# Transposes of two chunks moved from TensorE to VectorE and DRAM, in a rewritten instruction order

## The chip, the cores and the metric

The kernel runs on one core of a Trainium2 chip. The metric is the device time of one execution in microseconds (us). Three runs of the kernel before took 554.64, 554.66 and 555.55 us; their median is 554.66 us.

## The reference

Sequence length 2048, width 512, 32 heads of 16, hidden width 1376, everything in fp32. The block is an attention part followed by a mixing part:

```python
mod = silu(c) @ w_mod                      # six rows: sa, ca, ga, sb, cb, gb
h  = layernorm(x) * (1 + ca) + sa
q, k, v = split_heads(h @ wqkv)
phi(t) = [softmax(t @ w_phi), softmax(-t @ w_phi)]
o  = phi(q) (phi(k)^T v) / (phi(q) . sum(phi(k)))
x  = x + ga * (o @ wo)                     # called x2 below
h  = layernorm(x) * (1 + cb) + sb
g  = gelu(layernorm(h) @ w1)
x1 = h + shift(g) @ w2                     # quarters of g moved by +1, -1, +2, -2 rows
y  = x1 + gelu(layernorm(x1) @ w3) @ w4
out = x + gb * y
```

## The kernel before, in words

The 2048 rows are 16 tiles of 128 rows, and eight chunks (0 to 7) of two tiles each. A product of fp32 accuracy is made of three fp32r matmuls: every operand is split into a rounded part `hi` and a remainder `lo` (`hi_lo`, L483: one instruction makes `hi`, one subtraction makes `lo`), and `three` (L474) emits hi·hi, hi·lo and lo·hi.

There are three stages. First come the q, k and v projections of all rows, with the sums over k and v. Then `phase_a(c)` (L909) runs for each chunk: it finishes the attention, multiplies by `wo` (the pieces called o below: 6 matmuls of 128x512 for half of a tile), adds x, forms two layer norms with ScalarE (`moments`, `shift_of`), writes the normalized rows to the tile `n`, turns them with TensorE into the tile `nT` (`to_T`, L861), and multiplies `nT` by w1 (the pieces g: 24 matmuls of 128x256, two for each chunk). Its gelu goes to the tile `sh`, and `mix(c)` (L1009) multiplies shifted columns of `sh` by w2 (the pieces x: 3 matmuls of 128x512, four for each tile) and stores x1. Last come w3 and w4 in blocks of 512 rows (`block(s)`, L1208): the pieces u (6 or 12 matmuls) and v, and then the pieces b of `down_steps`.

`to_T` is where the change sits. For one tile of 128 rows it lets TensorE transpose four squares of 128x128 into one PSUM tile `pt` (`transp`, L477; matmuls of line L480) and makes `nT` from `pt` with `hi_lo`. The pieces n below are such sets of four transposes.

The stage of w3 already turns rows without TensorE: `normed(c)` (L1118) has ScalarE write the normalized rows with their columns permuted, VectorE transposes every 32x32 block of a tile (`turn`, L760), `store_rows` (L1103) puts the tile into a DRAM buffer, and `load_turned` (L1107) reads that buffer back with four DMAs, one for each group of 32 partitions, into the tile `bL`. Its line in the profile is L1111, that of the stores L1104.

Nothing schedules at run time. Each engine works off its instructions in order. The order comes from a list written out by hand into the file, `ORDER` (L40): it names 2801 planned operations by number, with a letter where an operation goes to another engine than its first (A ScalarE, V VectorE, G GpSimd). A second table, `SLOT` (L166), gives each tile its buffer. All DMAs quoted here are issued from one queue, SP, in the list's order; an issue that waits holds back all that stand behind it.

Read back into names, TensorE's part of the list around the change is this (chunk 5's pieces are g5, and the tiles 10 and 11 are its rows; chunk 6 has the tiles 12 and 13, chunk 7 the tiles 14 and 15; n12 and n14 name the transposes of chunks 6 and 7; x3 means three pieces in a row):

```
... x8 o14 u01 n10 x8 o14 o14 o14 | g5 n12 n12 g5 g6 g6 | x9 x10*3 x9*3 u00*2 x10 u00
    x11*4 u01 n14 n14 u01 v00 x12*2 g7 u02 g7 ...
```

Of the kernel before, what the change touches and what calls it, by code (L numbers as in the profile page):

```python
# [29 lines left out]
SHIFT = (1, -1, 2, -2)  # L30

# [9 lines left out]
    "0 3 35 6 52 2 42 50 5 54 56 36 237 23 7 37 11 1 12 13 14 17G 31 10 38 86G 19 39 43 88 8 44 18 9 49V 84 27 40 "  # L41
    "45 16 4 46 41V 51 47 87 53 48G 100 55 85G 92 15G 57 62 58 236 59 67 60 96 61 24 63V 68 81 64V 69 32 65V 70 "
    "151 20 239 33V 214 66 89 150 21V 28 90 34 332 22 101 230 29 25 30 93 227 238 26 216 97 240 71 241 225 102V "
    "82G 104 242 94V 243 153 95 83G 91 244 152 78 72 75 103 215G 113 246 233 106 154 98 248G 105 333 156 99 155 "
    "231V 107 157 334 311 219 140 158 245 316 217G 160 115 159 161 247V 79 162V 313 226G 114 228 412 168 142 163 "
    "169 218G 305 132 116 164 222 170 413 229G 165V 171 477 166 172 232G 117 167 254 73 249 141 335 80G 133V 300 "
    "255 769 195 135 109 76G 108 256V 143 220 312G 542 257 74G 478 134 144 110 182 145 136G 302 336 337 146 250V "
    "314 251V 173 184 338 221G 183 223 415 315 319 339 224G 185 301 203 252 174 77G 196 111 306 253 340 480 197 "
    "234 191 112G 198 303 204 118 258 342 317G 344 205 119 199G 341 268 138 343 120 479 308 206 318G 137 414 139 "
    "345 270 304G 350 416 259 346V 417 269 121G 201 175 320 347V 418 271 235G 208 127 200 351V 128 207 352V 321G "  # L50
    "202 193 786 261 353 176 419 787G 309 307G 788 354 177 543 260 178 209 420 186 348V 608 279 310G 481 679 179 "
    "422 421 482 424G 349 483 262 322 149G 423 187 122 323V 264 484 355 324 263 485 188 192 325 770G 487 486 545 "
    "180 773G 189 273 181G 326 265 123 396 544 489 430 357 124 194 356 190G 125 327 488 266 400 425 358 281 426 "
    "126 328 211 546 547 431 771 607 213G 777 129 610 282V 404 329 130 359 284 360 495 131V 490 272 267G 147 432V "
    "667 427V 148 408 210 283 428 212 361 491 285G 364 548 433 362 496 429 397G 774 434 792 789 286 435 405 287 "
    "775 549 492 288 274 550 609 776 409G 932 493 497V 552 275 373 554 790 276G 437 498 791 436 877 410 673 611 "
    "499 612 331 494 363G 444 551 398 365 553 366 367 399G 509 368 793 772 369 794 401 894 780 778 406 781G 438 "
    "613 881G 555 782 500 446 556 895G 445 557 878G 896 440 447 558 280 297 439 560 277 449 407 614 882 615 510 "
    "448 402 299 617 619 879 520 278 393 891 616 668 892G 370 618 411G 893 455 374 371 670 783 511 658 372G 824 "
    "897 521 441 561 562 512 883G 375 563 880G 1480 779 450 395G 502 442 625 564 620 626 296 559 403G 627 298 501 "  # L60
    "704 514 392 451 565 376 443G 621V 888 503 628 818 885 655 513 629 452G 674 504 394 567 622 505 474G 566 623 "
    "515 574 456 568 898G 624 569 886 900 1146 453 1247 576 671 887 901G 570 575 661 476G 330 516 506 630 571 "
    "889G 577 517G 639 507 578 454 508 579 539 518 572 541G 631 640 580 473 519 475 573G 702 705 538 540 385 641 "
    "675G 926 632 890 581 1140 633 604G 902 289 634 387 635 899 386 659 725 582G 642 884 662 731 388 644 377 660G "
    "643 636 390 606G 389 645 391 648 378 291 637 784 638G 379 785 290 585 380 649 795 703 653G 646 292 583 664 "
    "586 663 293 656 647 294 657 295 683 584 1481 381 684 797 603 685 605 672 383 652 457 708 1033 706 799G 458 "
    "650 709 707 665 382 460 669G 384 459 903 710 465 862 711 461G 651 712 713 714 796 717G 462 798 654 466 587 "
    "680 800 463 715G 464 467 718 801G 681 468 588 522 590 682 469G 716 802 905 719 523 720 907G 524 530 721 803 "
    "589 984 471 525 723 722 470 526G 804 472 908 732 531 805 533 591G 527 686 806 528 532 529 807 724 808G 592 "
    "906 593 594 733 904 687 810G 1001 1482 809 726 1004 1010 534G 734 727 689 735 688 736 812 728 536 694 909G "  # L70
    "811 737 738 739 729V 1005G 740 742 730 1007 535 741 744 813 690G 743 595 1012 816 814 695 745 910 666G 746 "
    "747 537 815 748 985G 676 817 819 749 1008G 911 691 1011 692 750 820 912 693 1014G 751 697 753 1039 913 696 "
    "825 752 914 757 821 1119 1002G 754 915 822 1015 758 916G 755 826 759 1003 756 1009 760 1006 918G 827 765 917 "
    "828 830 831 698G 919 832 920 833 835 1117 921 834 837 761 922 1016G 836 924 838 823 677 829 923 839 840 1013 "
    "1123G 699 927 841 1017 700 933 925 842 701 843 1018 1124 1226 986G 845 928 844 850 1019 988G 1020 1118 846 "
    "987G 851 1121G 852 847 1021 934 1224 848 853 849 1022 854 935 766 1023G 1122 762 763 929 936 1025G 1024 938 "
    "937 939 858 930 1120 767 931 764G 940 1026 998 768G 941 855 1027 943 1305 992 1028 942 945 865 1029 1228G "
    "1125 944 1031 866 596 1030 1386 867 856 1126 946 859 1034 857G 995 1032 860 1127 947 1128 861G 1040 949 1129 "
    "1091 1227 948 678G 1198 1041 1484 950 597 951 598 1035 1130G 1042 952 954 1229 953 868 958 1036 864 955 863 "
    "1132G 1043 871 869 956 959 1131 870 1045 972 1037 1047 1038 872 996G 957 1044 960 873 1133 599G 1486 1046 "  # L80
    "973 1048 1050 989 1388 974 1221 961 1049 1134 1052 993G 1135 975 1051 1230G 600 1053 601 874 1225 602 1054 "
    "966 1055 997 1108 1222G 1231 1136 1109G 1056 1223 1232 994 1483G 1138 1233 1234 962 1057 1235 999G 976 1307 "
    "1058 1236 1137 967 1239G 1387 968 1110 1060 1141 1059 1000 1114 1139 1061 977 1237G 875 1065 1147 1240 963 "
    "1111 1306 990G 1062 964 1066 1063 1487G 1148 991 1238 1215 876 1067 1092G 1142 1064 1112G 1068 1309G 1149 "
    "1113 1241 1253 1143 1242 1073 1308 1243 1245 1150 1216G 1244 1152 1151 1246 1093G 1566 1311 1217 978 1074 "
    "1069 1115 1094 1153 1154 1565 1116 965 1159 1155 1102 1156 1144 969G 1096 1160 1145 1248 1070 1583 1157 "
    "1097G 1075 1158 1071 1103G 1254 1098 1312 1161 1078 1162 1104 970 971 1622 979 1163 1072 980 1392 1567 1249 "
    "1164 1494 1165 1393 1218 1495G 1167 1255 1166 1568 1531 1310 1168 1219G 981 1250 1569 1076G 1099 1220 1169 "
    "1172 982 1079 1100G 1251 1170V 983 1080 1570 1313 1390G 1561 1314 1173 1171 1252 1081 1174 1101 1256 1571 "
    "1082 1315 1175 1186 1572 1584 1257 1316 1573 1623 1391 1180 1259 1077 1574 1485G 1576 1389 1261 1488G 1317 "  # L90
    "1575 1578 1318G 1577 1176 1083 1579 1586 1181 1260 1580 1266 1581 1258 1489 1585 1320 1514 1085 1084 1587 "
    "1588 1334 1086 1562 1262 1182 1187 1319 1263 1177 1192 1183G 1178 1321 1582 1087 1589 1179G 1188 1394 1563 "
    "1395 1264 1322 1492 1564G 1498 1323 1396 1397 1328 1088 1324 1516 1184 1326 1491G 1325 1189 1590 1398 1591 "
    "1089 1329 1490G 1593 1267 1090 1595 1399G 1327 1335 1592 1265 1500 1415 1594 1190 1268 1330 1270 1401G 1400 "
    "1191 1269 1193 1598 1271 1336 1272 1402 1599 1782 1499G 1331 1403 1337 1404 1493G 1506 1194 1273 1596 1409 "
    "1338 1185 1501G 1274 1332V 1597 1195 1340 1275 1405V 1781 1293 1279G 1496 1196 1294 1515G 1406 1197 1603 "
    "1295 1407V 1333 1600 1601 1276 1604G 1342 1408 1416 1784 1602 1341 1636 1339 1532 1343 1621 1783 1344 1345 "
    "1800 1280 1785 1517G 1347 1508 1296 1786 1346 1417 1281 1497G 1348 1787 1282 1410 1788 1277V 1278 1789 1349 "
    "1351 1350 1411 1297 1504 1298 1418 1791 1352 1793 1353 1412 1355 1354 1360G 1419V 1356 1413V 1518G 1283 1420 "
    "1790 1792 1796 1202 1361 1284 1794 1095G 1547 1357 1799 1421 1287 1362 1212G 1795 1105 1363 1285G 1358 1509 "  # L100
    "1359 1802 1549 1213 1106 1214 1364 1548G 1288 1797 1801 1107 1414 1286G 1803 1627 1804 1507G 1289 1368 1805 "
# [1286 lines left out]
```

## Time and profile before

| | |
|---|---|
| median of three runs | 554.66 us |
| profiled execution, whole | 554.69 us |
| profiled execution, span from first to last instruction | 552.9 us |
| TensorE matmuls | 544.9 us busy, 4498 instructions |
| VectorE | 488.6 us busy |
| ScalarE | 351.7 us busy |
| GpSimd | 344.5 us busy |
| bytes moved by DMA | 124.90 MB |

A matmul's busy time includes its latency, and neighbours overlap. So a run of matmuls is read from the start of one piece to the start of the next. The chain of waits gives such pieces back to back: start, length, engine, output tile, line, and the number of instructions. In the view of one tile, an answer gives minimum, median and maximum of a duration in ns; the line on landing gives minimum, median and maximum of the time from a DMA's issue to its completion in us.

### The profile page before, as it was taken

Reading aid. Unit: us, or ns where it says so; the run is one execution under the profiler, and the core shown is the slowest. Engines: PE = TensorE matmul, PEld = TensorE weight load, DVE = VectorE, ACT = ScalarE, POOL = GpSimd, SP = SyncE. Lnnn points to the kernel's source line nnn. Section 1 sums busy time; section 2 is a strip of 40 time slices with the busy share of each in tenths; the row PEclk is TensorE's granted clock in tenths of the full one; section 3 lists DMA queues with packets and bytes.
Section 4 is the critical chain, followed back from the end, with each engine's and each line's share of the span. In section 5 each row is a group of like instructions: output and inputs, shape, how many; then the busy total and the mean of one; then the engine's idle time right before and its main releaser. Section 6 shows DMA issues by size and latency. Waiting matters only on the chain.

```text
span 552.9 us, 12370 instructions
## 1 busy us (share of the span) xinstructions
PE 544.9 (99%) x4498; PEld 488.1 (88%) x4498; DVE 488.6 (88%) x903; ACT 351.7 (64%) x828; POOL 344.5 (62%) x351
## 2 busy tenths in 40 slices
PE   8999999999989999999999999999999999999997
PEld 7888788878767788888889898999999999999996
DVE  3999999899999999999998878987888868896886
ACT  2899898834436788969888877866434543434540
POOL 2499985979599999978886545234150434254442
PEclk9999999999999999999999999999999999999999
DMA  8982544537736766869987878986689673872022
GB/s 323 392 277 89 175 170 137 176 112 248 205 118 226 249 195 206 275 235 319 292 275 270 242 257 301 339 356 231 284 248 347 245 284 97 264 286 80 25 92 95
DMA packets 63749, 124.90 MB, mean 226 GB/s; under 512 B 7140, under 2 KB 26852, under 8 KB 59592
## 3 DMA queue, kind: packets, MB, share of 16 engines
q1 hardware_dynamic: 63400, 124.04, 66.4%
q8 instruction: 35, 0.57, 0.4%
q14 instruction: 26, 0.21, 0.1%
q10 hardware_dynamic: 288, 0.07, 0.1%
HBM read 89.74 MB, written 34.35 MB: 224 GB/s over the span
## 4 chain that ended last, share of the span: by engine, by line
PE 86%; DVE 7%; POOL 3%; DMA 2%; issue 1%; ACT 0%; DVEq 0%; POOLq 0%
PE pp L471 36%; PE pa L471 27%; PE ac L471 20%; PE pt L480 2%; DVE pz L442 2%; DVE q L442 2%; DMA mod<-in_wmod 1%; PE kva L471 1%; POOL qe L420 1%; DVE pT L762 1%; POOL ez L420 1%; POOL e L420 1%; DVE ez L418 1%; DMA const<-in_c 1%; DVE pp L437 0%
## 5 line engine op out<-in xcount | busy, mean ns | idle before, releaser
L471 PE MATMUL pp<-w,hh 128*128 128x512 f32 x576 | 138.8, 397 | 0.0
L471 PEld LDWEIGHTS pp<-w,hh 128*128 128x128 f32 x576 | 106.7, 188 | 26.1 <-issue 1.6
L471 PE MATMUL pa<-bH,wq 128*128 128x256 f32 x840 | 106.7, 281 | 0.0
L471 PE MATMUL ac<-w,gg 128*128 128x256 f32 x840 | 106.6, 281 | 0.0
L471 PEld LDWEIGHTS ac<-w,gg 128*128 128x128 f32 x840 | 103.4, 189 | 1.1
L471 PEld LDWEIGHTS pa<-bH,wq 128*128 128x128 f32 x840 | 103.1, 189 | 0.9
L471 PE MATMUL pp<-w,sh 128*128 128x512 f32 x192 | 49.4, 399 | 0.0
L471 PE MATMUL pa<-nT,w 128*128 128x256 f32 x384 | 48.3, 282 | 0.8 <-DVE nT L418 0.7
L471 PEld LDWEIGHTS pa<-nT,w 128*128 128x128 f32 x384 | 46.8, 188 | 2.5 <-DVE nT L418 1.2
L471 PE MATMUL pp<-w,oT 128*128 128x512 f32 x192 | 47.4, 395 | 0.0
L471 PEld LDWEIGHTS pp<-w,oT 128*128 128x128 f32 x192 | 35.4, 188 | 8.1 <-DVE oT L418 0.7
L401 ACT ACTIVATE gg<-cu 128x256 fp32r<-128x256 f32 (+1 forms) x56 | 19.1, 359 | 35.1 <-PE ac L471 19.7
L471 PEld LDWEIGHTS pp<-w,sh 128*128 128x128 f32 x192 | 34.6, 188 | 7.5 <-issue 0.8
L588 POOL TENSOR_TENSOR rs<-mv,const 128x2 f32<-128x2 f32 x31 | 23.8, 769 | 25.3 <-ACT mv L595 23.7
L401 ACT ACTIVATE cu<-pa 128x512 f32<-128x512 f32 (+1 forms) x42 | 21.5, 519 | 27.6 <-PE pa L471 22.3
L420 POOL TENSOR_TENSOR gg<-cu,gg 128x128 fp32r<-128x128 f32 (+1 forms) x26 | 15.8, 615 | 33.2 <-ACT gg L401 13.9
L420 POOL TENSOR_TENSOR ez<-e,const 128x1024 f32<-128x1024 f32 x12 | 29.2, 2433 | 5.2 <-DMA dram<-qe 5.1
L401 ACT ACTIVATE gg<-sg 128x512 fp32r<-128x512 f32 x38 | 23.1, 624 | 14.0 <-POOL sg L420 6.0
L420 POOL TENSOR_TENSOR e<-e,q 128x1024 f32<-128x1024 f32 x15 | 28.8, 1938 | 0.4 <-DVE q L418 0.2
L418 DVE TENSOR_TENSOR gg<-cu,gg 128x256 fp32r<-128x256 f32 (+1 forms) x54 | 22.1, 416 | 7.6 <-PE ac L471 4.6
L418 DVE TENSOR_TENSOR gg<-sg,gg 128x512 fp32r<-128x512 f32 x36 | 26.0, 722 | 3.0 <-PE ac L471 1.5
L420 POOL TENSOR_TENSOR ke<-ke,k 128x1024 f32<-128x1024 f32 x14 | 27.2, 1952 | 1.2 <-DVE k L445 1.2
(214 smaller groups left out, 1211.5 us busy)
## 6 DMA issues: line engine op xcount, KB each, us to landing
wq<-dram SPq DMA_DIRECT2D x32, 1024.0 KB, 7.8
dram<-ws SPq DMA_DIRECT2D x35, 256.0 KB, 3.1
xl<-in_x SPq DMA_DIRECT2D x32, 256.0 KB, 4.1
dram<-qe SPq DMA_DIRECT2D x16, 512.0 KB, 3.7
e<-dram SPq DMA_DIRECT2D x64, 128.0 KB, 3.2
raw<-in_w SPq DMA_DIRECT2D x18, 256.0 KB, 3.7
mod<-in_wmod SPq DMA_DIRECT2D x16, 256.0 KB, 5.2
dram<-xl SPq DMA_DIRECT2D x16, 256.0 KB, 3.0
```

The costliest lines, as they stand in the source:

```text
L401: nc.scalar.activation(o(), i(), func, **kw)
L418: dve = ("DVE", 71 + 1.04 * o.n + 90 * (isps(a) and isps(b)), lambda: nc.vector.tensor_tensor(o(), a(), b(), op=op))
L420: pool = ("Pool", cost, lambda: nc.gpsimd.tensor_tensor(o(), a(), b(), op=op))
L442: plan.op("DVE", 65 + 1.04 * a.n + 110 * isps(o), lambda: nc.vector.tensor_reduce(o(), a(), axis=AX.X, op=op), [o], [a])
L471: nc.tensor.matmul(o(), a(), b(), start=s, stop=e, **kw)
L480: nc.tensor.transpose(o(), i(), ident())
L588: plan.op("Pool", 540 + 10 * m, lambda: nc.gpsimd.tensor_tensor(r(), v(), mhalf[:, :m](), op=OP.pow), [r], [v, mhalf])
L762: plan.op("DVE", 71 + 1.04 * o.n, lambda: nc.vector.transpose(o(), i()), [o], [i])
```

## The change

`FAR = (6, 7)` names the two last chunks of `phase_a`. For these, and for no other chunk, `to_T` is not called. ScalarE writes the rows of a tile with permuted columns, VectorE turns the 32x32 blocks (`turn`), the tile is stored to DRAM, and once both tiles are stored four DMAs load the block rows back into a tile `bL`; two `hi_lo` then make `nT` from `bL`, one for two of its four column groups each. `store_rows` and `load_turned` are moved up in the file unchanged.

```diff
+FAR = (6, 7)
...
             nm, r = moments([hs[t] for t in ts_], tot, [ns[t] for t in ts_])
             nmr = shift_of(nm, r)
+            far = c in FAR
             for i, t in enumerate(ts_):
-                act(ns[t], hs[t], scale=r[:, i:i + 1], bias=nmr[:, i:i + 1])
+                x, o = hs[t], ns[t]
+                if far:
+                    x, o = (v.re(pat, (NK, NK, 32), j=32, k=NK) for v, pat in ((x, "p (k b j) -> p k b j"), (o, "p (b k j) -> p k b j")))
+                act(o, x, scale=r[:, i:i + 1], bias=nmr[:, i:i + 1])
                 sl = slice(t * P, (t + 1) * P)
-                to_T(ns[t], nT[:, 0, :, sl], nT[:, 1, :, sl])
+                if far:
+                    y = T("yt")
+                    turn(y, ns[t])
+                    if i == 0:
+                        yd = T("dram", [TPC * P, D])
+                    store_rows(yd, t, y)
+                else:
+                    to_T(ns[t], nT[:, 0, :, sl], nT[:, 1, :, sl])
+            if far:
+                z = T("bL", [P, CH // 32, NK, 32])
+                load_turned(z, yd)
+                for k in (0, 2):
+                    hi_lo(*(nT[:, i, k:k + 2, :].re("p k (a j) -> p k a j", (2, CH // 32, 32), j=32) for i in range(2)),
+                          z[:, :, k:k + 2, :].perm("p a k j -> p k a j", (1, 0, 2)), lo_eng="any", alts=("DVE",))
```

`ORDER` (now 2807 operations) and `SLOT` are replaced as a whole. Of the operations that both lists hold, 246 go to another engine than before, most of them between VectorE and GpSimd in both directions. Up to the w1 pieces of chunk 1, TensorE's pieces behind the q projections stand in the same order as before. Around the two chunks the new list reads, for TensorE:

```
... n10 x8 n10 x8 o14 x8 x8 o14 o14 | g5 g5 u01 u01 x9 x10 g6 x9*3 u00 x10 g6
    x11 u00 v00 x10*2 u01 x11*3 u00 x12*4 g7 g7 u02 ...
```

The u01 that stood ahead of g5 stands behind it. The second layer norm of a chunk begins behind its two instructions with output `h` (VectorE, L437). For chunk 6, the second of them stands in the old list between the first and the second of the last three o14; in the new list it stands between the first x8 and the second n10 of this excerpt. For chunk 7 it stands in the new list ahead of the last x9. VectorE's part of the new list, from the end of chunk 6's second layer norm on (each line is one instruction):

```
turn of tile 12
turn of tile 13
lo of bH from bL (for the w3 stage)
lo of nT of chunk 5, second tile
...
hi of nT of chunk 6, column groups 2 and 3      (waits for the block loads)
hi of a w3 product (ws)
lo of nT of chunk 6, column groups 2 and 3
lo of sh of chunk 5
lo of nT of chunk 6, column groups 0 and 1      (ScalarE makes their hi)
```

On SP the new list has the stores of the two turned tiles, two loads of xl, a load of raw, then the four block loads of chunk 6, and behind them the store of x2 of tile 15, a store of turned rows of the w3 stage, a store of ws, another store of turned rows, and a load of wq. For chunk 7 the block loads stand behind the two stores of turned rows, a store of ws, a load of raw and a load of xl. In the new list chunk 7's tiles come in the order 15, 14 up to the loads.

More of the change, by code (lines that the diff above doesn't have):

```diff
@@ L177 @@
-    "xn": "ab75aj6ejag7f54b",
-    "mod": "ekbk73e1dj930hf2ke",
+    "pp": "423510426361520134360643057536624547376626100253031152670367136713526741237522437454617155647742"
+          "1327761503062143013",
+    "bd": "68",
+    "w": "134625cd180395ace127b3",
+    "rk": "52937cgb",
+    "xl": "01jif4ac4k9iah0gi1fjhk8d9b366bkf4lf0hi08i21bk43b",
+    "st": "01b8h03f90aei13bgj4b25c9e5i60g13e",
+    "mv": "25fa268cj68ch0aei13d38ififhj4j97c",
+    "rs": "36gc1aed1579j68ch0ajfeg7be12ahfab",
+    "nm": "47ei9dj45b7gih243bfgd2457f9d268g47abd3c67c90h158d20458i6",
@@ L179 @@
+    "xn": "ae95dkhgf807e5lj",
+    "mod": "d0126l7ed73ecg0l21",
     "mod2": "1023",
     "kva": "4",
-    "za": "7",
-    "hh": "0789abe0",
-    "pt": "71713064136760724740255030200105",
-    "raw": "948hcla7b2l2g59fd34940abi351",
-    "k1": "0110502430210140",
-    "ke": "4501639451823940",
-    "k2": "5343025543253140",
-    "vv": "3246ekjhkfh0170l",
-    "qe": "7692282134682731",
-    "q1": "3242123515032015",
-    "qt": "ajj9ib759209",
-    "acc": "clf1e",
-    "kvs": "1",
-    "pz": "1",
@@ L195 @@
-    "q2": "03105351",
-    "e": "5617956458034928",
-    "ez": "4988322399990775",
-    "q3": "1245243214024032",
-    "q5": "44423145",
-    "pT": "3044399695373795",
-    "oT": "4a4ea04b",
-    "nT": "b05444be",
-    "n": "l12l4aaf1h5kje7g",
-    "h": "7519l62c7i1lfkcd",
-    "gf": "21535500",
-    "sh": "92be2cb0",
-    "pa": "720435033552357536277143075740636220453477601263027041460272",
-    "wr": "80061",
-    "ws": "010ie23c3782d1hgibgibgfbd0id69267k7",
-    "gb": "8",
-    "tw": "08935",
@@ L224 @@
-    "xc": "5le904k6jhi2fg2i",
-    "uu": "00k2i6ck",
+    "za": "0",
+    "hh": "0789abe7",
+    "pt": "0757121717505257414263566463",
+    "raw": "8f3h681ka5gld206ehd34dg9jae1",
+    "k1": "0154033234514253",
+    "ke": "4598637458213749",
+    "k2": "1421410203014143",
+    "vv": "4dl2e3266k8ii46c",
+    "qe": "7602221830231860",
+    "q1": "3202505212350312",
+    "qt": "108k0546gjdi",
+    "acc": "bj15f",
+    "kvs": "a",
+    "pz": "0",
+    "q2": "03125415",
+    "e": "5687452763540123",
@@ new lines @@
+    "ez": "4026611504115886",
+    "q3": "1245043013203240",
+    "q5": "44405142",
+    "pT": "3908640216481802",
+    "oT": "46bea7b6",
+    "nT": "a75bbeeb",
+    "n": "0cl00l6lg02lj0jf",
+    "h": "4gc25kj8ac51l638",
+    "gf": "19646023",
+    "sh": "426e767b",
+    "pa": "151231654605013045226176041704252664712745305326040673256044",
+    "wr": "19997",
+    "ws": "ci6b674f4f5he21iafa25ei1h04a20f2cb4",
+    "yt": "2jk4l2f03jkfk2j2c45k",
+    "bL": "2346930816",
+    "gb": "7",
+    "tw": "53517",
@@ new lines @@
+    "nb": "beeiebibc4c4j6k8",
+    "bH": "81283402681457299547702120351531",
+    "tr": "k0kihgalhf6gcf5f",
+    "wq": "b42648d60486d04680d460d4860d64d6048d",
+    "cu": "h5glfd02b8e463bi5a0hd4hg9063ckgh286c1ifa",
+    "gl": "62gb5dd2",
+    "ac": "26530325430634725361137256031742",
+    "gg": "87541827057024691584617532476165398107452638079835794827098276450912386079125843",
+    "sg": "c1e1hh1g1jl89fdjc28j52c8ca2ij539lj39a50g",
+    "xb": "i9kc20lfe1b4elkh",
+    "xc": "5c189881k4a8l83j",
+    "uu": "j19blf9d",
@@ L907, in q_phi, with store_rows, load_turned, fn @@
         return turned
+    def store_rows(dst, t, i):
+        plan.op("SP", 475, lambda: nc.sync.dma_start(dst()[t * P:(t + 1) * P, :], i()), [dst[:, t * P:(t + 1) * P]], [i],
+                lat=P * D * 4 / 380., land=1500 + P * D * 4 / 300.)
+    def load_turned(o, src):
+        def fn():
+            for b in range(NK):
+                nc.sync.dma_start(o()[32 * b:32 * (b + 1)].rearrange("p a k j -> p a (k j)"),
+                                  src().rearrange("(a i) (b f) -> b i a f", i=32, b=NK)[b])
+        plan.op("SP", 4 * 475, fn, [o], [src], lat=QB * D * 4 / 380., land=4500)
     def phase_a(c):
@@ L1101, in body @@
     load_w4_last()
-    def store_rows(dst, t, i):
-        plan.op("SP", 475, lambda: nc.sync.dma_start(dst()[t * P:(t + 1) * P, :], i()), [dst[:, t * P:(t + 1) * P]], [i],
-                lat=P * D * 4 / 380., land=1500 + P * D * 4 / 300.)
-    def load_turned(o, src):
-        def fn():
-            for b in range(NK):
-                nc.sync.dma_start(o()[32 * b:32 * (b + 1)].rearrange("p a k j -> p a (k j)"),
-                                  src().rearrange("(a i) (b f) -> b i a f", i=32, b=NK)[b])
-        plan.op("SP", 4 * 475, fn, [o], [src], lat=QB * D * 4 / 380., land=4500)
     GROUPS = ((0, 2), (2, 4), (4, 5))
```

22 lines of the change are left out of this document (removed), and 248 rows, old and new, of the table ORDER.

## The prediction

> **What bounds the kernel now.** I read the busy shares first, then the chain of waits, then TensorE's waits, then the stage in which the change lies. From the page, TensorE and its granted clock:
>
> ```profile
> span 552.9 us, 12370 instructions
> PE 544.9 (99%) x4498; PEld 488.1 (88%) x4498; DVE 488.6 (88%) x903; ACT 351.7 (64%) x828; POOL 344.5 (62%) x351
> PEclk9999999999999999999999999999999999999999
> PE 86%; DVE 7%; POOL 3%; DMA 2%; issue 1%; ACT 0%; DVEq 0%; POOLq 0%
> ```
>
> TensorE is the bound by sum and by chain. From 205 us on it waits for nobody: the windows (length, then busy time of PE, PEld, DVE, ACT, POOL, then clock, DMA share, GB/s) show it busy for 344 of 344 us. The four waits below are its whole list for the span, 4.1 us, and they lie ahead of that.
>
> ```profile
> 205.00:549.00 344.00, 344.00 (x2833) 325.49 (x2831) 297.45 (x611) 213.10 (x518) 179.88 (x227) 1.00 0.70 238
> ...
> PE pp L471 <- DVE pT L762: 1.7, 1, 1.7
> PE pp L471 <- POOL const L498: 1.0, 1, 1.0
> PE pp L471 <- DMA mod<-in_wmod: 0.7, 1, 0.7
> PE pa L471 <- DVE nT L418: 0.7, 1, 0.7
> ```
>
> So behind 205 us every piece that TensorE loses is time won, and every wait it gains is time lost, one for one.
>
> **The change, part by part.** The chain of waits around chunks 6 and 7 gives the pieces and their prices:
>
> ```profile
> 284.30 1.44 PE pa L471 x12
> ...
> 291.00 2.83 PE pa L471 x24
> 293.82 0.87 PE pt L480 x8
> 294.70 8.57 PE pa L471 x72
> ...
> 310.32 0.70 PE pp L471 x3
> 311.01 1.42 PE pa L471 x12
> 312.44 2.78 PE pp L471 x12
> 315.21 0.71 PE pa L471 x6
> 315.92 0.87 PE pt L480 x8
> ...
> 321.02 7.16 PE pa L471 x60
> ```
>
> *Removed.* The two pieces of eight transposes, at 293.82 and 315.92: 2 x 0.87 = 1.74 us of a TensorE that is never idle there. That is the whole gain; the number of hi and lo instructions stays (two of each for a chunk), and PSUM merely gets two tiles free.
>
> The Trainium skill advises the opposite way (VectorE: DVE Perf Modes, "Rules for kernel authors"): a 128x128 transpose belongs on TensorE where a PSUM result will do. Its 390 ns for one (section "The three transpose paths") would make sixteen worth 6.2 us; the rows say 0.87 us for eight, so the sum goes by 1.74.
>
> *Added, off the path.* Four turns on VectorE, priced by the same operation on the w3 stage's rows; four stores and eight block loads on SP:
>
> ```profile
> L762 DVE STREAM_TRANSPOSE yt<-nb x16: 668/704/712, 261.3 to 377.5; 128x512 f32<-128x512 f32 x16
> DMA to landing us min/median/max: 2.0/2.9/6.4
> 301.06 1.80 SPq L1111 DMA_DIRECT2D bL<-dram x4
> DMA to landing us min/median/max: 2.4/3.2/6.2
> 300.00:320.00 20.00, 20.00 (x135) 18.32 (x134) 16.71 (x32) 17.62 (x44) 10.49 (x15) 1.00 0.86 265
> ```
>
> (The first landing line is that of the stores of yt, the second that of the loads of bL.) The turns are 4 x 0.70 = 2.8 us; VectorE has 3.3 us free in the 20 us quoted last, so its sum doesn't set the end. Four loads take SP 1.80 us to issue. The 2 MB of extra traffic on 124.90 MB cost nothing by themselves: TensorE hides them as long as the operands arrive in time. If that cover is gone, the price is the lateness below.
>
> *Added, on the path: is chunk 6's nT in time?* I put both kernels on the clock of the one before. These rows tell how long the second norm takes (the second h, and the norms behind it) and what VectorE does behind it:
>
> ```profile
> 286.60 0.74 DVE L437 SCALAR_TENSOR_TENSOR h<-pp,rs,const 128x512 f32<-128x512 f32 x1
> ...
> 291.42 0.82 ACT L401 ACTIVATE n<-h,nm,rs 128x512 f32<-128x512 f32 x1
> ...
> L418 DVE TENSOR_TENSOR bH<-bL,bH x13: 677/685/1052, 283.0 to 509.3; 128x512 fp32r<-128x512 f32 x13
> ```
>
> Due. Chunk 5's first w1 piece starts at 291.00; the u01 of 1.44 ahead of it goes behind, so it starts at 289.6. Up to chunk 6's first piece come two w1 pieces (5.7), two u01 (2.9), x9 and x10 (1.4): due at 289.6 + 10.0 = 299.5.
>
> Ready. Before, the second h starts at 286.60, 4.4 us ahead of the w1 piece, and by the list it stands two to three o14 (2.8 to 4.2 at 0.23 us a matmul) ahead of it. In the new list n10, three x8 and three o14 lie behind it, 6.7 us, and part of another x8. I take 7.1: it starts at 282.5. From its end to the end of the last norm it is 292.24 - 287.34 = 4.9 us, so the norm ends at 288.1. The second turn ends at 288.9. Its store is issued at 289.0 and lands 2.9 us later, at 291.9. Then the four loads: the last is issued 3/4 of 1.80 later, at 293.3. The landing of all 32 such loads has its middle at 3.2 us (above); the groups of four that are nearest in the program are less even:
>
> ```profile
> L1111 SPq DMA_DIRECT2D bL<-dram x4: 319/465/501, 282.3 to 283.7; - x4
> DMA to landing us min/median/max: 4.0/4.0/4.0
> L1111 SPq DMA_DIRECT2D bL<-dram x4: 319/445/449, 301.1 to 302.4; - x4
> DMA to landing us min/median/max: 5.9/6.1/6.2
> L1111 SPq DMA_DIRECT2D bL<-dram x4: 318/443/449, 350.1 to 351.5; - x4
> DMA to landing us min/median/max: 5.4/5.6/5.8
> ```
>
> The group of 6.1 has a load of wq (1 MB) right ahead of it on SP; in the new list xl, xl and raw (256 KB each) stand there, as around the 4.0. I take 4.0: landed at 297.3. VectorE then works off five instructions in a row (four of 0.6 to 0.68, and one of half their columns, 0.3): 300.1. That is 0.6 to 0.7 us late. The bounds: stores of 2.0 and loads of 2.4 leave nT 1.8 us early; stores of 6.4 and loads of 6.2 make it 6.4 us late.
>
> A second wait hides in the same queue. The lo of chunk 5's nT stands on VectorE behind both turns, and so behind chunk 6's norm: 288.9 plus two subtractions of 0.6 is 290.1, for a piece due at 289.6. These 0.5 us are no addition; they are the first part of the 0.7. While VectorE waits for the loads, the lo of sh of chunk 5 is queued behind it, for which x10 waits: it costs nothing beyond either, since x10 stands next to g6.
>
> *Chunk 7.* Its loads are measured from chunk 6's second w1 piece, E. The second h stands about 3.2 us ahead of E by the list; 0.74 for itself and 4.9 for the norm, with 0.5 more for two other ScalarE instructions between, end it at E + 3.0. Turn and issue 0.8, store 2.9, issue 1.4, landing 4.0 and three VectorE instructions of 2.0: E + 14.1. Due: the piece itself 2.85, then x11, u00, v00, two x10, u01 (6 matmuls), three x11, u00 (6) and four x12, which at 0.70, 1.44, 1.42, 1.40, 0.71, 2.1, 0.71 and 2.8 make E + 14.1. On time to a tenth, so every tenth of lateness counts. By the bounds it is 2.5 early or 5.7 late.
>
> *The list elsewhere.* Up to chunk 1, TensorE's pieces behind the q projections have the old order, so the waits listed above stay; VectorE's part is only shuffled. I put it at 0, with 0.7 either way, the size of the small waits above.
>
> Sum: -1.74 + 0.7 + 0 + 0 = -1.0 us. The profiled execution took 554.69 (552.9 of span and 1.8 around it), 0.03 above the median: 553.7.
>
> **The rivals.**
>
> *Hidden wholly.* Norm, stores and loads run half a microsecond ahead of my sum, as they do with landings of 3.2: both chunks on time, 554.7 - 1.74 = 552.9. For it: 3.2 is the middle of all such loads. Against: nT of chunk 5 has to wait behind the turns whatever the loads do.
>
> *The round trip paces TensorE: slower.* The place is SP's block loads, and TensorE's wait at the first w1 piece of chunks 6 and 7. If they land in 5.85, the mean of the two slow groups quoted, both chunks come 1.85 later: waits of 2.5 and 1.9, -1.74 + 4.4 = +2.7, 557.4. It decides from a landing of 4.5 on (0.7 + 2 x 0.5 = 1.7 takes the gain), and shows as slower from 5.1. For it: DMA engines 86% busy, and the 1.7 us wait of the first numerator on the turned tile of the same kind of round trip. Against: no 1 MB load directly ahead.
>
> *Nothing to measure.* The rewritten list loses the rest of the gain elsewhere by some wait of 0.7 to 1: 554.7. For it: 246 operations on other engines. Against: TensorE lost nothing behind 205 us with the old list.
>
> *The clock drops.* If chunk 6 came later still, TensorE could fall to a lower clock: a store of 6.4 and loads of 6.2 make one gap of 6.4 us, and 554.7 - 1.74 + 6.4 = 559.4 already without that. The granted clock shows no dip in any of the 40 slices quoted, the one with the 1.7 us wait among them. The Trainium skill (TensorE: Matmul & The Clock Gate, "Why this matters for your kernels") warns of idle gaps over some 3 us, behind which the array runs at half clock; by its window of 3.4 us another 1.7 would come on top. No row here has such a gap.
>
> **How the numbers follow.** My forecast (553.3 to 554.6 by itself) 0.41, hidden 0.22, nothing to measure 0.12, the slower round trip 0.23, the clock 0.02. 0.2% is 1.1 us, about what a measurement of this kernel can tell from no change. The forecast's centre lies just inside that bound and half of its chance beyond: faster is 0.22 + 0.20 = 0.42; same 0.12 + 0.21 = 0.33, slower 0.25. Range 552.4 (all hidden, and 0.5 won elsewhere) to 557.2, which leaves out the end of the slow case and the clock.
>
> **What would show it.** Sixteen transposes of n fewer on TensorE, 48 of them left. In the chain, pieces back to back between chunk 5's and chunk 7's w1; any gap ahead of the first pa<-nT of chunk 6 or 7, put down to the lo or hi of nT, is my 0.7 and its fate. The first pa<-nT of chunk 5 waiting for its lo shows the turns' queue. Landings of the new bL loads near 4.0 support the sum; 3.2 or less means the hidden case, over 5 the slow one. It is wrong in kind if the time moves while TensorE shows no gap in 285 to 325 us and no fewer transposes.

## The result, and the profile after

The changed kernel takes 558.1 us (median of five runs, 556.9 to 559.3) against 555.0 us (median of five, 554.6 to 555.6): a ratio of 1.0059, with a 95% interval of 1.0045 to 1.0073. It is slower by 0.6%, where 553.7 us were forecast, and 557.2 was the top of the forecast's range. Its runs scatter by 2.4 us, those of the kernel before by 0.9. The profiled execution took 557.9 us, 3.2 more than the one of before, and its span shows the same 3.2.

The page of the changed kernel, its whole list of TensorE's waits, and the window from 205 to 549 us that was shown of before:

```profile
span 556.1 us, 12353 instructions
PE 544.8 (98%) x4482; PEld 487.1 (88%) x4482; DVE 492.1 (88%) x895; ACT 353.1 (64%) x836; POOL 350.2 (63%) x355
PEclk9999999999999999999999999999999999999999
205.00:549.00 344.00, 341.75 (x2803) 322.18 (x2803) 300.80 (x608) 214.28 (x522) 186.47 (x230) 1.00 0.74 244
PE pa L472 <- DVE nT L419: 1.7, 3, 0.8
PE pp L472 <- DVE const L419: 1.4, 1, 1.4
PE pp L472 <- ACT kvs L402: 1.3, 1, 1.3
PE pp L472 <- POOL const L499: 1.0, 1, 1.0
PE pp L472 <- DVE q L419: 1.0, 1, 1.0
PE pp L472 <- DMA mod<-in_wmod: 0.7, 1, 0.7
PE pp L472 <- DVE oT L419: 0.6, 2, 0.4
```

The sixteen transposes are gone (4482 matmuls instead of 4498). But four waits of before, 4.1 us, have become ten, 7.7 us, and TensorE now loses time behind 205 us, where it lost none. None of the new waits is for the turned rows: kvs, const and q belong to the attention, and of the three waits for nT two are those of chunks 0 and 1. The third is chunk 5's, which has a share in the change.

Where the time goes is read from the start of the same piece in both kernels. First before, then after (start, length, pieces, and in brackets the idle time ahead and its releaser):

```profile
154.14 3.05 PE L471 MATMUL pp<-w,hh 128*128 128x512 f32 x12
157.12 0.66 PE L471 MATMUL pp<-const,kvs 128*64 128x128 f32 x8
...
162.47 1.16 PE L471 MATMUL pp<-pT,const 64*32 64x128 f32 x64 [1.72 <-DVE pT L762]
...
203.45 6.31 PE L471 MATMUL pa<-nT,w 128*128 128x256 f32 x48
```

```profile
154.16 3.05 PE L472 MATMUL pp<-w,hh 128*128 128x512 f32 x12
158.48 0.67 PE L472 MATMUL pp<-const,kvs 128*64 128x128 f32 x8 [1.27 <-ACT kvs L402]
...
163.55 1.16 PE L472 MATMUL pp<-pT,const 64*32 64x128 f32 x64 [1.41 <-DVE const L419]
...
204.76 0.28 PE L472 MATMUL pa<-nT,w 128*128 128x256 f32 x1
205.47 5.90 PE L472 MATMUL pa<-nT,w 128*128 128x256 f32 x47 [0.43 <-DVE nT L419]
...
271.03 1.67 PE L472 MATMUL pp<-w,sh 128*128 128x512 f32 x6
273.65 0.71 PE L472 MATMUL pp<-w,oT 128*128 128x512 f32 x2 [0.96 <-DVE q L419]
274.76 1.19 PE L472 MATMUL pp<-w,oT 128*128 128x512 f32 x4 [0.39 <-DVE oT L419]
...
293.42 0.28 PE L472 MATMUL pa<-nT,w 128*128 128x256 f32 x1
294.16 5.84 PE L472 MATMUL pa<-nT,w 128*128 128x256 f32 x47 [0.46 <-DVE nT L419]
...
304.09 3.01 PE L472 MATMUL pa<-nT,w 128*128 128x256 f32 x24
...
325.22 4.95 PE L472 MATMUL pa<-nT,w 128*128 128x256 f32 x40
```

At 154 us both are level. The first numerator piece starts 1.1 later, the second matmul of chunk 1's w1 piece some 1.9 later (203.45 + 0.12 against 205.47). At 0.23 us a matmul, six and two of them should take 1.4 and 0.5 from 271.03 on; the next pieces come 1.2 and 0.6 later than that. Chunk 5's w1 loses 0.6 behind its first matmul. That is 1.9 + 1.8 + 0.6 = 4.3 of new loss against the 1.74 that the transposes gave: +2.6, and 0.6 of the 3.2 lies in smaller shifts. Of the 4.3, 3.7 lie ahead of 291.43 us, where the first turn of the change runs (next view), so the turned rows can't have caused them. Chunks 6 and 7 (304.09 and 325.22) start without any wait.

The change itself, on VectorE and on the load queue of the changed kernel (the landing lines belong to the loads named above them):

```profile
291.43 1.50 DVE L763 STREAM_TRANSPOSE yt<-n 128x512 f32<-128x512 f32 x2
...
293.43 0.68 DVE L419 TENSOR_TENSOR nT<-pt,nT 128x512 fp32r<-128x512 f32 x1
...
302.41 0.69 DVE L419 TENSOR_TENSOR nT<-bL,nT 128x512 fp32r<-128x512 f32 x1
L918 SPq DMA_DIRECT2D bL<-dram x4: 319/446/452, 295.1 to 296.5; - x4
DMA to landing us min/median/max: 3.4/3.9/4.1
L918 SPq DMA_DIRECT2D bL<-dram x4: 319/442/451, 316.2 to 317.5; - x4
DMA to landing us min/median/max: 4.5/4.7/4.8
```

From the end of the second turn (292.9) to the last lo of chunk 6 (303.1) it is 10.2 us; the prediction had 288.9 to 300.1, 11.2. The lo of chunk 5 (293.43) stands behind the two turns, as foretold.

### The profile page after: what moved, and what is told of

Same layout as the page of the kernel before. It is cut to its first block, busy times and chain, and to the rows that moved or that the text cites. A ratio compares the mean times of both kernels' runs of the same rounds, so it can differ in the third digit from the quotient of the medians.

```text
span 556.1 us, 12353 instructions
## 1 busy us (share of the span) xinstructions
PE 544.8 (98%) x4482; PEld 487.1 (88%) x4482; DVE 492.1 (88%) x895; ACT 353.1 (64%) x836; POOL 350.2 (63%) x355
## 5 line engine op out<-in xcount | busy, mean ns | idle before, releaser
L421 POOL TENSOR_TENSOR gg<-cu,gg 128x256 fp32r<-128x256 f32 (+1 forms) x32 | 22.7, 714 | 30.9 <-ACT gg L402 12.8
L402 ACT ACTIVATE cu<-pa 128x512 f32<-128x512 f32 (+1 forms) x39 | 19.7, 512 | 30.9 <-PE pa L472 15.5
L402 ACT ACTIVATE gg<-cu 128x256 fp32r<-128x256 f32 (+1 forms) x63 | 21.1, 354 | 17.1 <-PE ac L472 12.7
L419 DVE TENSOR_TENSOR gg<-sg,gg 128x512 fp32r<-128x512 f32 x34 | 24.8, 731 | 5.5 <-PE ac L472 2.6
L419 DVE TENSOR_TENSOR cu<-pa,cu 128x512 f32<-128x512 f32 (+1 forms) x36 | 21.3, 597 | 6.0 <-PE pa L472 4.6
```

The source lines that it names most:

```text
L402: nc.scalar.activation(o(), i(), func, **kw)
L419: dve = ("DVE", 71 + 1.04 * o.n + 90 * (isps(a) and isps(b)), lambda: nc.vector.tensor_tensor(o(), a(), b(), op=op))
L421: pool = ("Pool", cost, lambda: nc.gpsimd.tensor_tensor(o(), a(), b(), op=op))
```

## The experiments

Ratios are to the kernel before on the same chip, with 95% intervals; 2.3 us of a median are 0.0041.

| run | what it is | median us | ratio |
|---|---|---|---|
| after | the changed kernel | 558.1 | 1.0059 (1.0045 to 1.0073) |
| list_only | new list, change out, first form | 581.3 | 1.0484 (1.0467 to 1.0502) |
| list_only2 | new list, change out, second form | 561.1 | 1.0121 (1.0106 to 1.0135) |
| old_then_new | old list to 284 us, then new | 582.3 | 1.0490 (1.0473 to 1.0508) |
| window | old, new from 240 to 335 us, old | 556.0 | 1.0028 (1.0017 to 1.0040) |
| window_pe | as window, change out | 558.4 | 1.0069 (1.0048 to 1.0090) |
| old_start | old to 175 us, then new | 555.8 | 1.0022 (1.0013 to 1.0030) |
| start60 | first 60 entries old | 557.7 | 1.0055 (1.0036 to 1.0075) |
| w7_moved | one VectorE operation moved | 557.2 | 1.0046 (1.0033 to 1.0060) |
| w7_kvs | the same, and kvs moved | 557.6 | 1.0046 (1.0025 to 1.0067) |
| slot_n10 | two tiles in other buffers | 558.1 | 1.0073 (1.0050 to 1.0097) |
| mended | old_start, three operations moved | 556.3 | 1.0032 (1.0020 to 1.0045) |
| mended2 | old_start, 33 operations moved | 555.9 | 1.0017 (1.0007 to 1.0027) |

The theory: the pieces of the change were sized about rightly, and the new list loses the rest in places that have nothing to do with the turned rows. The rival: the turns and their round trip through DRAM cost it.

### The change taken out of the new list

```diff
-FAR = (6, 7)
+FAR = ()
 ORDER = (
...
-turns, stores and block loads of chunks 6 and 7
+four pieces of transposes: chunk 6's where its last store stood, chunk 7's in the stretch behind x11
+(list_only2: chunk 7's a little earlier); hi and lo behind them
```

> The new list and its buffers, with the change itself taken out: both tiles of chunks 6 and 7 are turned by TensorE again, their transposes standing where the last store of chunk 6 and the stretch behind x11 of chunk 7 stood, so sixteen transposes are back and no turn, store or block load of the normalized rows is left. Theory (the list elsewhere costs it: waits of TensorE at 157 to 163, at 203 and at 271 to 275 us, 1.3, 0.5 and 1.9 us by the two traces, none of which touches the turned rows): the two pieces of eight transposes come back (2 x 0.87 = 1.74) and the 0.6 of chunk 5's late lo goes, so 558.1 + 1.74 - 0.6 = 559.2, a ratio to the kernel before of about 1.008, and the waits at 157 to 275 are all there. Rival (the turns and the round trip cost it): with them gone the time is back at 555, ratio 1.000.

It took 581 us, against both. The waits between 157 and 275 us were there as in the changed kernel, but 13 us went at 324, 382 and 445 us. The two longest waits, 6.0 and 4.6 us, are for the tiles uu and cu of the last stages; ahead of them ScalarE stands still for stores:

```profile
386.53 0.38 ACT L401 ACTIVATE uu<-ac 128x256 f32<-128x256 f32 x1 [10.31 <-DMA dram<-yt]
...
447.90 0.60 ACT L401 ACTIVATE cu<-pa 128x512 f32<-128x512 f32 x1 [13.04 <-DMA out_dram<-xb]
```

In this form the normalized tiles of chunk 7 are kept longer, and some 50 tiles behind them got other buffers, down to the last stage. Neither uu nor cu is made from what these stores write; a store holds them up only where they take over the stored tile's buffer. The granted clock also fell behind them (mean 0.988). So this run tells of buffers, not of the change. The second form frees the tiles sooner.

> The new list without the change, as in the run list_only, but with both transposes of a chunk put where its tiles come free at once, so that only 25 or so tiles change buffer and no projection waits for a buffer of the last stage. Theory (the list elsewhere): 558.1 + 1.74 - 0.6 = 559.2, ratio 1.008, with the waits at 12, 158, 163, 205 and 271 to 275 us as in the changed kernel. Rival (turns and round trip): 555, ratio 1.000.

It took 561.1 us, with the waits at 158, 163, 205 and 271 to 275 us as in the changed kernel. The rival's 555 is out: without the turned rows the new list is 6.1 us slower than the kernel before, and with them 3.4 less (0.0121 - 0.0059 = 0.0062, some 2.3 to 4.6 us; the two ratios come from different sets of runs). The theory had 559.2, and what the 1.9 above it are is not shown: this form, too, has over 40 tiles in other buffers, and in its profiled execution, the slowest with 563.4 us, a part is a lower clock, told below.

### The change alone, in an order nearer to the old one

```diff
 ORDER = (
-new list
+old list, first 1395 entries (old_then_new), or first 1140 (window, window_pe)
+what is left of the new list (window, window_pe: only of its first 1700 entries)
+what is left of the old list (window, window_pe)
...
-FAR = (6, 7)
+FAR = ()                                     (window_pe)
```

In all of these the buffers are given out anew.

> The list and the buffers of the kernel before up to chunk 7's first product with wo (some 284 us), and from there the new list with the turned rows of chunks 6 and 7. Theory (the list elsewhere): no late piece at 157 to 163, 203 and 271 to 275; the sixteen transposes are gone, -1.74, and the lo of chunk 5's nT costs 0 to 0.6, so 554.7 - 1.74 + 0.3 = 553.3, between 552.9 and 553.6, ratio 0.997. Rival (turns and round trip cost it): 557 or more, ratio over 1.003, with waits of TensorE behind 284 us.

582 us, against both. At the seam, operations that the new list has done earlier all come behind 284 us. TensorE's first waits behind it are 1.5 and 3.3 us for nT of chunk 5. Most tiles behind the seam are in other buffers, and ScalarE stood 17.6 us, in three waits, for stores of xb ahead of cu, as in the run list_only. It tells nothing of the change.

> The change with as little of the new list as it takes: the list of the kernel before up to the n8 stage (some 240 us), the new list from there to the l4 and x12 stages (some 335 us) with the turned rows of chunks 6 and 7, and behind them the order of before again; buffers given out anew for this order, none of n's to follow a stored tile closely. Theory (the pieces of the change were sized rightly, the list elsewhere cost the rest): 16 transposes gone, -1.74; chunk 5's lo behind the turns, +0.6; nothing at 12, 158, 163 and 271 to 275 us: 555.0 - 1.1 = 553.9, ratio 0.998. Rival (the turns, the stores and the block loads cost more than the transposes wherever the list stands): 556 to 558, ratio 1.002 to 1.006, with TensorE's waits at or behind 293 us.

> The same order as in the run window, but with the change taken out: the rows of chunks 6 and 7 are turned by TensorE, transposes and their hi and lo put where the turns, stores and first hi stood. Theory: the difference to window is the change alone, +1.74 - 0.6 = +1.1, so 555.0, ratio 1.000. Rival (the round trip costs more than it saves): faster than window by 1 to 3 us, 553 to 555, and window's extra waits gone.

By itself, 556.0 is the number of window's rival. But with the same order 556.0 stands against 558.4 us: the kernel with the turned rows is the faster by 0.0041, some 0.9 to 3.6 us. In the profiled executions it is 0.9 (spans of 554.1 and 555.0), near the 1.1 expected; the kernel with transposes scattered more, from 556.8 to 561.7. So the change gains, as far as other buffers leave the two comparable, and the rival is out a second time. But neither kernel comes out where the theory put it: they are 2.1 and 3.4 us slower than expected, so the new order from 240 to 335 us, with its buffers, costs 2 to 3 us by itself. In the run window TensorE's new losses there are 0.5 at 271 (oT), 0.7 at 278 (pT) and 0.6 at 291 us; the last is chunk 5's lo and belongs to the change.

The windows from 280 to 320 us of before, after, window and window_pe, in this order (DMA share and GB/s stand last):

```profile
280.00:320.00 40.00, 40.00 (x269) 36.70 (x268) 35.76 (x64) 35.77 (x92) 26.68 (x33) 1.00 0.83 264
```

```profile
280.00:320.00 40.00, 39.54 (x312) 35.08 (x311) 35.89 (x69) 33.05 (x86) 23.71 (x35) 1.00 0.94 295
```

```profile
280.00:320.00 40.00, 39.52 (x257) 35.63 (x257) 36.31 (x68) 32.24 (x83) 22.37 (x31) 1.00 0.92 285
```

```profile
280.00:320.00 40.00, 39.72 (x262) 35.80 (x261) 32.12 (x62) 31.87 (x83) 21.09 (x29) 1.00 0.73 230
```

In the same order the turned rows raise the DMA engines' share from 0.73 to 0.92. The order matters as well: the kernel before has 0.83 without turned rows. That share is what the change pays with: the round trip fits, but the stretch has little room left for a late transfer.

### Where the list loses: the first 175 us

```diff
 ORDER = (
-new list
+old list, first 820 entries (old_start), or first 60 (start60)
+what is left of the new list
```

> The changed kernel with the order of before up to some 175 us (through den0 and the first num piece) and the new list from there, turned rows included; buffers given out anew. Theory: the losses of the start (0.2 to 1.3 at 12 us by the profiles so far) and of 158 to 163 us (1.1) go, the one of 271 to 275 may go too, since the buffers are other ones: 558.1 - 1.5 to - 3.4, so 554.7 to 556.6, ratio 0.9995 to 1.003. Rival (the losses there are made up by waits behind them anyhow): 558, ratio 1.005.

> The changed kernel with the first 60 entries of its list in the order of the kernel before (the first loads, the modulation matmuls, the first two transposes), the rest and all buffers as in the changed kernel. Theory (the new order of the first loads makes the modulation matmuls wait for in_wmod, 1.8 to 2.6 us in the runs with the new start against 0.3 to 1.1 with the old one): TensorE's first projection comes 0.2 to 1.3 earlier, but since the wait at 163 us is for VectorE's chain, part of it is lost there again: 558.1 - 0.3 = 557.8, between 557.0 and 558.1, ratio 1.005. Rival (the start is worth all of what the run old_start won): 556, ratio 1.002.

With the old order to 175 us the time is 555.8, some 2 us (0.0037) better than the changed kernel. The first 60 entries alone, with every buffer unchanged, give 557.7: 0.0004, nothing that can be told. In the profiles TensorE waits 0.7 to 2.6 us for in_wmod with the new start and 0.2 to 1.1 with the old one, 0.7 in the changed kernel and in the one before. These overlap, so what the start is worth is not shown; most of what old_start won came later, or from its buffers.

```diff
 ORDER = (
...
-... 663 603 685 605 383 708 652 665 457 797 382 672 706 ...
+... 663 603 685 605 383 672 708 652 665 457 797 382 706 ...        (w7_moved, w7_kvs)
...
-... 717G 463 798 462 654 466 464 587 800 1146 680 ...
+... 717G 798 654 466 587 800 1146 680 463 462 464 ...              (w7_kvs)
```

Operation 672 is the second lo of w7, 708 and 706 are the products ez of chunk 0; 680 copies kvs, and 463 and 462 make qe of tile 8 on ScalarE; 464 moves with them.

> The changed kernel with one VectorE operation moved: the second lo of w7 (128x512, 0.69 us where it stood in the kernel before, 2.90 us beside GpSimd's ez now) goes ahead of the first product ez of chunk 0, where it stood before. Theory (that operation delays the two ez products and so pT of the first num piece; TensorE waits 1.41 for it at 163.5): the pT chain ends 1.2 earlier, 558.1 - 1.1 = 557.0, ratio 1.0037, num's first piece starts at 162.5 instead of 163.55. Rival (kvs, which stands behind both exps on ScalarE in the new list, decides at 158.5, and the chain behind it is as late without the moved operation): 558 and the gaps at 158 and 163 unchanged in sum.

> The changed kernel with w7's second lo ahead of chunk 0's ez on VectorE, as in the run w7_moved, and kvs ahead of the two copies of qe of tile 8 on ScalarE, as in the kernel before. Theory (both together are what the stretch of 158 to 163 us costs): no wait for kvs, num's first piece 1.1 earlier: 558.1 - 1.2 = 556.9, ratio 1.0035. Rival (the chain of pT decides alone, and the moved operation of w7 has won what is to be had): as w7_moved, 557.2, ratio 1.0046. Rival 2 (TensorE only arrives earlier at the waits of 271 to 293 us): 558, ratio 1.0055.

What stood in the way is plain in the rows. VectorE and GpSimd of the changed kernel, then VectorE and TensorE of the run w7_kvs:

```profile
145.45 2.90 DVE L419 TENSOR_TENSOR w<-raw,w 128x512 fp32r<-128x512 f32 x1
...
144.54 3.26 POOL L421 TENSOR_TENSOR ez<-e,const 128x1024 f32<-128x1024 f32 x1 [4.24 <-DMA dram<-qe]
```

```profile
143.44 1.28 DVE L418 TENSOR_TENSOR w<-raw,w 128x512 fp32r<-128x512 f32 x2
...
162.15 1.16 PE L471 MATMUL pp<-pT,const 64*32 64x128 f32 x64 [1.17 <-DVE const L418]
```

The subtraction takes 0.6 where it runs alone and 2.90 beside GpSimd's product: it ends half a microsecond behind the end of that product (147.80). The Trainium skill says why this can be (SBUF — State Buffer, "Who interferes with whom"): VectorE and GpSimd share one pair of ports under an exclusive lock. The row agrees. The numerator piece now starts at 162.15 in the profile of w7_kvs, where the changed kernel had 163.55, and the wait for kvs is gone: 1.4 us, where 1.1 to 1.2 were expected. The whole profiled execution is 1.5 shorter (span 554.6). The medians don't settle it: w7_kvs, with runs from 555.8 to 560.1, shows 0.5 and has the same ratio as w7_moved, 1.0046, which is what its rival had. Nor does the profile of w7_moved: its first projection starts 1.2 later than that of the changed kernel (21.16 against 19.94), and the numerator at 163.18.

### Where the list loses: 271 us

```diff
 SLOT = {
-    "raw": "8f3h681ka5gld206ehd34dg9jae1",
+    "raw": "8f3h681ka5gld206ehd2ldg9jae1",
-    "n": "0cl00l6lg02lj0jf",
+    "n": "0cl00l6lg034j0jf",
...
 ORDER: the loads 1504 and 1506 stand behind the store 1084
```

The later tenants of these four buffers change places with them.

> The changed kernel with the squares of chunk 5's two tiles (n of the wo stage) in buffers last held by an x tile and a tile that ScalarE read, not in those of two stored yt tiles; two prefetched loads of w41 change places with them and stand two places later in SP's queue. Theory (the wait of 2.33 us on ScalarE for the store of yt at 269.4 delays the normalization of chunk 5's rows and oT, and with it TensorE by 0.96, 0.39 and the rest up to 1.9): 558.1 - 1.9 = 556.2, ratio 1.0024, and the gaps at 273.7 and 274.8 gone. Rival (TensorE was going to wait there anyhow, for q or oT, whose VectorE work is late for other reasons): 557.5 or more, ratio 1.005.

The wait is gone, the time is not. ScalarE of the changed kernel, then VectorE and TensorE of slot_n10:

```profile
269.38 0.69 ACT L402 ACTIVATE n<-pp,nm 128x512 f32<-128x512 f32 x1 [2.33 <-DMA dram<-yt]
```

```profile
286.55 0.75 DVE L437 SCALAR_TENSOR_TENSOR h<-pp,rs,const 128x512 f32<-128x512 f32 x1 [1.03 <-DMA dram<-xl]
...
294.79 1.45 PE L471 MATMUL pa<-nT,w 128*128 128x256 f32 x10 [1.00 <-DVE nT L418]
```

In the changed kernel the square of chunk 5's first tile goes into the buffer of a turned tile whose store is still under way, and everything behind it on ScalarE stands for 2.33 us. With another buffer TensorE passes 271 to 275 us without a gap. But now ScalarE stands 1.31 for a load of xl at 281.85, behind the moved loads, and VectorE 1.03 for a store of xl: two tiles h have changed buffers too, and this wait lies ahead of chunk 6's second norm. So the turns come later, chunk 5's lo stands behind them, and TensorE waits 1.0 for it instead of 0.46. Of the gain 0.6 is left by the profiles (the numerator of slot_n10 starts 1.1 later, and its span is 0.5 longer), and nothing by the medians. The rival was right on the total and not on its reason: most of what was won went to the next transfers for which ScalarE and VectorE wait.

### Three waits mended at once

```diff
 ORDER = (                                     (from old_start)
+1327 ahead of 1267   (second lo of chunk 6's oT)
+1405 ahead of 1602   (turn of pT15)
+1282 ahead of 1357   (lo of chunk 5's nT, ahead of the two turns)
```

> The kernel of the run old_start with three VectorE operations moved: the second lo of chunk 6's oT ahead of two others (TensorE waited 0.24 for it at 271 us), the turn of pT15 ahead of two operations of the w3 stage and wo's residual (0.52 at 278 us), and chunk 5's lo of nT ahead of the two turns of the change (0.48 at 291 us). Theory (each of these waits is decided by what stands ahead on VectorE): 555.8 - 0.4 - 0.6 - 0.6 = 554.2, ratio 0.9987, faster than the kernel before. Rival (the wait moves on: TensorE comes earlier to chunk 6's first hidden piece, whose lo came 0.7 before it at 301.95, and waits there for the block loads): 555.2, ratio 1.0005.

> The kernel of the run old_start with 33 operations of VectorE, ScalarE, GpSimd and the store queue between some 245 and 335 us moved by up to 25 places, TensorE's order and all buffers kept: the lo of chunk 5's nT and of g5's sh earlier, copies of the weights' preparation later, chunk 5's squares and sums earlier. Theory: as mended, and the hi and lo of chunk 6's nT start earlier too, so the wait does not move on: 554.2, between 553.6 and 555, ratio 0.9987. Rival (what is moved later is missed by the stages behind it): 555.8 or more, ratio 1.002.

TensorE in the run mended:

```profile
290.30 5.92 PE L471 MATMUL pa<-nT,w 128*128 128x256 f32 x48
...
300.29 0.28 PE L471 MATMUL pa<-nT,w 128*128 128x256 f32 x1
300.73 3.04 PE L471 MATMUL pa<-nT,w 128*128 128x256 f32 x23 [0.16 <-DVE nT L418]
...
322.14 0.38 PE L471 MATMUL pa<-nT,w 128*128 128x256 f32 x1
322.87 5.80 PE L471 MATMUL pa<-nT,w 128*128 128x256 f32 x47 [0.34 <-DVE nT L418]
...
339.92 0.36 PE L471 MATMUL pa<-bH,wq 128*128 128x256 f32 x1 [0.59 <-ACT w L401]
```

The hi on VectorE, ahead of chunk 7's piece:

```profile
320.61 0.43 DVE L410 TENSOR_SCALAR nT<-bL 128x512 fp32r<-128x512 f32 x1 [0.57 <-DMA bL<-dram]
```

The three waits are gone: chunk 5's w1 runs through from 290.30, where old_start began at 291.25 and lost another 0.6. But 556.3 is no better than 555.8. TensorE is 1.6 us ahead of old_start at chunk 5's w1 (0.4 of it already at the first numerator piece) and 0.6 behind at 341 us. Of these 2.2 us the starts place 0.3 at chunk 6, 0.6 at chunk 7 and 0.6 at 340 us; the rest lies in smaller shifts. The first two are the rival's mechanism, and the first is what is left of the prediction's own 0.7: once TensorE is on time, it waits for the turned rows. The third, for w, has nothing to do with them, and the rival's 555.2 was not met either. The wider rearrangement of mended2 gave 555.9, as its rival had it (555.8 or more): in its profile TensorE still waits 0.5 for chunk 5's lo. No kernel run here beats the one before.

## Why the prediction was wrong

The sum was -1.74 + 0.7 + 0 + 0 = -1.0, and +3.1 came out.

*Removed, -1.74.* Right as far as it could be tested: sixteen transposes are gone, and taking the change out costs 0.9 (profiles) to 2.3 us (medians) in the run window and 3.4 in the new list, where the two terms of -1.74 and 0.6 would leave 1.1. The rule of the Trainium skill that the prediction weighed (VectorE: DVE Perf Modes, "Rules for kernel authors"), transposes on TensorE, did not pay here: with TensorE as the bound, the run window, with VectorE's turns, was faster than window_pe by 0.9 to 3.6 us.

*Chunk 6, +0.7, and chunk 5's lo in it.* The lo waited behind the turns for 0.46 us by the list of waits, 0.6 by the starts, where 0.5 had been foretold. The four loads landed in 3.4 to 4.1, for which 4.0 was taken. The second half of the term did not show, because TensorE came 4.6 us later to chunk 6 than reckoned (304.09 against 299.5) and the last lo only 3.0 later: the chain from the turns to this lo took 10.2 instead of 11.2, and the wait for chunk 5's lo had come first. In mended, where TensorE is early, it shows as 0.3.

*Chunk 7, 0.* No wait, with loads of 4.5 to 4.8 and lo some 0.6 ahead of the piece; 0.6 of wait in mended.

*The list elsewhere, "I put it at 0, with 0.7 either way".* This is the step that failed. In the places read above it measured +3.7 (the 4.3 without the 0.6 of chunk 5's lo), and by the run list_only2 the new list alone, with that run's buffers, costs 6.1. The argument was that TensorE's pieces keep their order up to chunk 1, so that the waits there stay, and that VectorE's part is only shuffled. But 1.9 of the 3.7 fell in just that stretch, up to 205 us. A shuffle of VectorE, ScalarE and buffers is enough to set TensorE's waits: kvs came 1.27 us late with TensorE's order unchanged. Behind 205 us TensorE had not a single wait, which says that every operand came in time, not that it came with room; no row was read for how early operands were. The term's width was taken from the waits that were seen, and these were what was left after the old list had hidden the rest. The rival *Nothing to measure* named this mechanism and gave it 0.7 to 1 us and a chance of 0.12.

*The round trip paces TensorE.* It was not the cause of the slowdown: chunks 6 and 7 start without a wait. It is one of the next bounds, as mended shows: 0.9 of the 2.2 us lost again there. The repair of slot_n10 was lost at other transfers.

Of the new list's loss these runs place some 1.4 us at 158 to 163, in one profile, and 1.8 at 271 to 275, which moved on when mended. That the order from 240 to 335 us, with its buffers, costs 2 to 3 us by itself is shown by the run window_pe; how much of that is needed to make room for the round trip was not separated. Nor was order separated from buffers: the new list came with a new table of buffers, and the runs old_start, window and window_pe each have their own.

## What to carry to other kernels

When a change comes with a new order, price the order as a part of its own: look up, for each engine and buffer, how long before its use an operand was ready, since a bound engine without waits shows nothing of that room. Test it by taking the change out of the new order, and by moving as few buffers as possible; the two longest waits of list_only, over 10 us of TensorE together, stood behind buffers that stores still held. And expect repaired waits to reappear at the next operand that comes just in time, so count a repair by the time of the whole.

## What the runs showed of the hardware that was not expected

*A store can take long to land.* The stores of turned tiles in the changed kernel, min, median and max of the whole span:

```profile
L911 SPq DMA_DIRECT2D dram<-yt x20: 319/320/863, 263.2 to 382.2; - x20
DMA to landing us min/median/max: 2.0/2.6/10.6
```

Before, the longest was 6.4. A buffer that is read by such a store is free only when it has landed; two of these tiles are followed by ScalarE's squares, and one of these waited 2.33 us.

*The clock fell behind waits of under 2 us.* In the profile of list_only2 the waits at 271 us were 1.44 and 0.41, a little longer than the 0.96 and 0.39 of the changed kernel. TensorE's pieces of list_only2, and the granted clock around them (it stands ahead of the last two columns):

```profile
274.81 0.70 PE L471 MATMUL pp<-w,oT 128*128 128x512 f32 x2 [1.44 <-DVE q L418]
275.92 1.50 PE L471 MATMUL pp<-w,oT 128*128 128x512 f32 x4 [0.41 <-DVE oT L418]
```

```profile
272.00:276.00 4.00, 2.16 (x9) 1.14 (x8) 2.39 (x6) 3.90 (x10) 2.00 (x3) 1.00 0.64 183
276.00:280.00 4.00, 4.00 (x11) 3.15 (x12) 3.69 (x8) 3.43 (x8) 4.00 (x3) 0.58 0.88 319
```

TensorE was busy for 2.16 of 4 us, and then the clock was 0.58 over the next four. In the changed kernel the same four held 2.65 busy, and the clock stayed at 1.00. The Trainium skill (TensorE: Matmul & The Clock Gate, "Why this matters for your kernels") warns of idle gaps over some 3 us; here two shorter ones, with 0.7 of work between them, were enough. A single wait of 2.39 us in list_only, with 1.61 busy of the four from 324 to 328 us, left it at 1.00, so these runs don't give the rule; but a wait that grows by half a microsecond can cost more than itself. The wider scatter of the runs with the new list is mostly something else: the slowest of slot_n10 (561.2) and of start60 (561.1) had a mean granted clock of 1.00.
